# Mixer halves of the first two output row tiles computed ahead of the attention halves

## The chip, the core and the metric

The kernel runs on one core of a Trainium2 chip. The metric is the time of one execution on the device, in microseconds (us); lower is better. TensorE (PE) multiplies matrices and writes its results into PSUM, which this kernel uses as eight banks of 128 x 512 float32. VectorE (DVE) and ScalarE (ACT) read PSUM and work on tiles in SBUF, the on-chip memory. SyncE's queue (SP) issues all the transfers of the part that matters here. PEld in the profile is TensorE loading the stationary operand of the next matmul.

## The reference

A sequence of 2048 rows of width 1024 goes through two branches, and a gate for each row mixes them:

```
g = sigmoid((x * gate_w).sum(-1))                 # one number for each row
a = attention(x) @ wo                             # 32 heads of 32, 8 keys at distance 2
z = gelu(x @ w_in)                                # 3584 columns, halves z1 and z2 of 1792
b = (z1 * (w_sp @ layernorm(z2) + b_sp)) @ w_out
out = g * a + (1 - g) * b
```

The inputs and the output are bfloat16. The attention of a row sees itself and seven earlier rows, 2, 4, ... 14 back.

## The kernel before

The kernel writes its instructions in an order that is laid down by hand; each engine works through its own list in that order, and semaphores hold an instruction until what it reads is there. The PE work comes in stages: z2 for the gate and layer norm (L232), the queries, keys and values (L447), z1 (L483), and then the stages around the change.

`g_chunk(c)` (L491 to L505) computes the spatial mixing for a chunk of 512 rows: for each of 14 feature tiles 16 matmuls into a bank `ps` (L497), a copy by ACT into one of three `gsb` buffers (L501), the bias added and the product with z1 taken by DVE (L502, L503). The product replaces z1 in the tile `z1c`, of which there are two, for even and odd chunks.

`final_chunk(c)` (L507 to L533) makes the output of the four row tiles `a` of 128 rows in a chunk. For each half of 512 columns it runs the **attention half**, 8 matmuls of the transposed attention output `oT` with `wo` into a bank `psa` (L519), and then the **mixer half**, 14 matmuls of `z1c` with `w_out` into a bank `psb` (L523). ACT scales psa by the gate into `asb` (L526), DVE adds psb times one minus the gate (L527), and the finished row tile is stored (L533). All banks come from one pool of eight under one tag. There are three `oT` buffers; `load_oT(a + 2)` (L369) is issued when row tile `a` begins, and the first three are loaded before the stage.

The attention runs on DVE, beside PE's matmuls, in eight groups of four heads. A small planner called `Beat` counts PE's columns as time and puts DVE's attention steps and some transfers in between by due times: `beat.run(cols)` advances its clock and issues what has come due, and `beat.flush(t)` issues all that is due up to t. The last steps of the attention in that plan are: the store of the last two head groups into the scratch tensor `o_d` in device memory (`store_o`, L326), the four loads of `wo` (`load_wo`, L366), and the first three transposed reads of `o_d` into the `oT` buffers.

The end of the program is written out as

```
g_chunk(0)
...
g_chunk(1)
...
beat.flush(1e9)
final_chunk(0)
load_z1c(2)
g_chunk(2)
final_chunk(1)
load_z1c(3)
g_chunk(3)
final_chunk(2)
final_chunk(3)
```

Here `load_z1c(c)` (L400) reads the z1 of a chunk into its tile, and `load_wsp` (L397) the spatial weights of a chunk, into one of two buffers. `w_out` is read by one transfer ahead of `g_chunk(0)` (L539).

Of the kernel before, what the change touches and what calls it, by code (L numbers as in the profile page):

```python
# [10 lines left out]
F32 = mybir.dt.float32  # L11
BF = mybir.dt.bfloat16

P = 128
S = 2048
D = 1024
KT = D // P
# [9 lines left out]
NF = FH // P  # L27
# [24 lines left out]
def kernel(  # L52
# [13 lines left out]
    nc = tc.nc  # L66
# [5 lines left out]
    psum = ctx.enter_context(tc.tile_pool(name="psum", bufs=8, space=bass.MemoryType.PSUM))  # L72
# [4 lines left out]
    def reg(off, n):  # L77
        return arena[:, off:off + n]
# [20 lines left out]
    for jh in range(2):  # L99
        for w in range(W):  # L100
            n = min(8, max(0, 14 - 2 * w - 8 * jh))
            if n > 0:
# [3 lines left out]
    g_s = sm.tile([P, 16], F32, name="g_s")  # L106
    gl_s = sm.tile([P, 16], F32, name="gl_s")
    omg = sm.tile([P, 16], F32, name="omg")
# [17 lines left out]
    w_out_sb = reg(X_OFF, NF * D).rearrange("p (f n) -> p f n", f=NF)  # L126
# [5 lines left out]
    wo_sb = reg(A_OFF, KT * D).rearrange("p (k n) -> p k n", k=KT)  # L132
    oT_slots = [reg(A_OFF + 8192 + r * 1024, 1024).rearrange("p (k t) -> p k t", k=KT) for r in range(3)]
    ob_slots = [reg(A_OFF + 11264 + r * 1024, 1024) for r in range(3)]
    asb_slots = [reg(A_OFF + 14336 + r * 1024, 1024).bitcast(F32) for r in range(2)]
# [10 lines left out]
    z1c_slots = [reg(CD_OFF + 8192, 7168).rearrange("p (f t) -> p f t", f=NF),  # L146
                 reg(EF_OFF + 8192, 7168).rearrange("p (f t) -> p f t", f=NF)]
# [49 lines left out]
    beat = Beat()  # L197
# [170 lines left out]
    def load_oT(a):  # L368
        sync.dma_start_transpose(oT_slots[a % 3], o_d[a * P:(a + 1) * P, :])  # L369
# [26 lines left out]
    def load_wsp(c, aa):  # L396
        sync.dma_start_transpose(wsp_slots[c % 2][:, :, aa, :], wsp_v[4 * c + aa])  # L397
# [41 lines left out]
    for ch in range(NCH):  # L439
# [3 lines left out]
        for j in range(NJ):  # L443
            ps = psum.tile([P, 512], F32, name="ps", tag="ps")
            for kt in range(KT):
                lhsT = _sub_ap(xT_flat, kt * S + j, [[NJ, P]])
                nc.tensor.matmul(ps[:].rearrange("p (t c) -> p t c", t=4), lhsT, wgt[:, :, kt, :],  # L447
                                 start=(kt == 0), stop=(kt == KT - 1))
# [25 lines left out]
    for f in range(NF):  # L474
# [5 lines left out]
        for c in range(4):  # L480
            ps = psum.tile([P, 512], F32, name="ps", tag="ps")
            for kt in range(KT):
                nc.tensor.matmul(ps[:], w1[:, kt, (f % 4) * P:(f % 4 + 1) * P], xT[:, kt, 512 * c:512 * (c + 1)],  # L483
                                 start=(kt == 0), stop=(kt == KT - 1))
# [6 lines left out]
    def g_chunk(c):  # L491
        wsp = wsp_slots[c % 2]
        z1c = z1c_slots[c % 2]
        for f in range(NF):
# [9 lines left out]
            beat.on_vector(0.85)  # L504
            beat.run(16 * 512)  # L505

    def final_chunk(c):  # L507
        z1c = z1c_slots[c % 2]
        for aa in range(4):
            a = 4 * c + aa  # L510
            oT = oT_slots[a % 3]
            ob = ob_slots[a % 3]
            if a > 0 and a + 2 < 16:
                load_oT(a + 2)
            last = a == 15
            for n0, nw in ((0, 512), (512, 256), (768, 256)) if last else ((0, 512), (512, 512)):
                psa = psum.tile([P, 512], F32, name="psa", tag="ps")
                for kt in range(KT):
                    nc.tensor.matmul(psa[:, 0:nw], oT[:, kt, :], wo_sb[:, kt, n0:n0 + nw],  # L519
                                     start=(kt == 0), stop=(kt == KT - 1))  # L520
                psb = psum.tile([P, 512], F32, name="psb", tag="ps")
                for f in range(NF):
                    nc.tensor.matmul(psb[:, 0:nw], z1c[:, f, aa * P:(aa + 1) * P], w_out_sb[:, f, n0:n0 + nw],  # L523
                                     start=(f == 0), stop=(f == NF - 1))
                asb = asb_slots[n0 // nw % 2][:, 0:nw]
                nc.scalar.activation(asb, psa[:, 0:nw], ACT.Copy, scale=g_s[:, a:a + 1])  # L526
                nc.vector.scalar_tensor_tensor(ob[:, n0:n0 + nw], psb[:, 0:nw], omg[:, a:a + 1], asb,  # L527
                                               ALU.mult, ALU.add)
                beat.run((KT + NF) * nw)
                if last:  # L530
                    sync.dma_start(out2[a * P:(a + 1) * P, n0:n0 + nw], ob[:, n0:n0 + nw])
            if not last:
                sync.dma_start(out2[a * P:(a + 1) * P, :], ob)  # L533
# [9 lines left out]
    g_chunk(1)  # L543
    for aa in range(4):
        load_wsp(3, aa)
    beat.flush(1e9)
    final_chunk(0)
    load_z1c(2)
    g_chunk(2)
# [6 lines that stand above are left out]
# [29 lines left out]
```

## Time and profile before

| what | value |
|---|---|
| median of 3 runs | 720.5 us (719.03 to 721.43) |
| profiled execution, its own time | 722.27 us |
| span of the profiled execution | 720.5 us |
| mean granted TensorE clock | 0.995 |
| PE busy | 711.8 us, 99% of the span |
| DVE, ACT busy | 413.7 us, 246.3 us |
| matmuls of g_chunk (L497) | 896, 193.9 us |
| attention halves psa (L519) | 264 in the records, 62.3 us |
| mixer halves psb (L523) | 462 in the records, 103.4 us |

The profile records one execution. The span goes from its first to its last instruction; the execution's own time also holds what lies around the span. The table of groups gives for each kind of instruction how many there were, their busy time, the mean of one, and the idle time of the engine just before them with what ended it. The chain of waits is followed back from the last instruction, at each step to what released it. The granted clock is 1.00 at full speed.

### The profile page before, as it was taken

The page shows a single profiled execution, that of the slowest core. Times are in us where ns is not written, and L with a number is a line of the kernel's source. Part 1 is how long each engine was busy: PE and PEld are TensorE (multiplying, and loading weights), DVE is VectorE, ACT ScalarE, POOL GpSimd, SP SyncE. Part 2 cuts the span into 40 slices and gives each one's busy share as a digit, 9 for nine tenths or more (in the row PEclk, how much of TensorE's full clock was granted, in tenths as well). Part 3 has the DMA queues.
Part 4 walks back from the last instruction along what each step waited for, and adds up shares of the span by engine and source line. Part 5 has one row for each costly group of instructions (what it writes and reads, how often), then busy time and mean ns, then how long its engine had stood idle before and what let it go on. Part 6 is the DMA issues. An engine that isn't in the chain of part 4 may idle for free. (4 is left out here: it accounts for less than half of the span.)

```text
span 720.5 us, 8378 instructions
## 1 busy us (share of the span) xinstructions
PE 711.8 (99%) x3372; PEld 365.8 (51%) x3372; DVE 413.7 (57%) x429; ACT 246.3 (34%) x451; POOL 14.0 (2%) x23
## 2 busy tenths in 40 slices
PE   8999999999999999999999999899999999999998
PEld 4466666666655554444444444344444444444444
DVE  0000589999999999999999999311222112221111
ACT  4433544435379885343421211111112111111111
POOL 1000000000000212000000000000000000000000
PEclk9999999999999999999999999999999999999999
DMA  9984974876672035955369580862400113002310
GB/s 234 191 180 106 250 199 110 200 182 171 177 229 82 0 114 120 258 199 172 142 195 313 189 172 1 226 139 58 132 1 0 42 47 131 1 1 58 60 45 30
DMA packets 176759, 92.89 MB, mean 129 GB/s; under 512 B 145104, under 2 KB 166992, under 8 KB 176208
## 3 DMA queue, kind: packets, MB, share of 16 engines
q1 hardware_dynamic: 176720, 92.36, 48.0%
q8 instruction: 26, 0.43, 0.2%
q14 instruction: 13, 0.11, 0.0%
HBM read 47.71 MB, written 28.38 MB: 106 GB/s over the span
## 5 line engine op out<-in xcount | busy, mean ns | idle before, releaser
L497 PE MATMUL ps<-arena 128*128 128x512 bf16 x896 | 193.9, 379 | 0.0
L447 PE MATMUL ps<-arena 128*128 128x512 bf16 x768 | 165.9, 379 | 0.0
L497 PEld LDWEIGHTS <-arena 128*128 128x128 bf16 x896 | 87.7, 98 | 105.7
L447 PEld LDWEIGHTS <-arena 128*128 128x128 bf16 x768 | 110.7, 144 | 55.1
L523 PE MATMUL psb<-arena 128*128 128x512 bf16 (+1 forms) x462 | 103.4, 376 | 0.0
L275 DVE TENSOR_TENSOR arena<-arena 128x8192 bf16<-128x8192 bf16 x16 | 70.8, 4424 | 51.9 <-DMA arena<-k_d 51.6
L527 DVE SCALAR_TENSOR_TENSOR arena<-psb,omg,arena 128x512 bf16<-128x512 f32 (+1 forms) x33 | 24.2, 735 | 131.9 <-PE psb L523 131.9
L232 PE MATMUL ps<-arena 128*128 128x512 bf16 (+1 forms) x512 | 97.3, 352 | 1.1 <-DMA arena<-in_B_w_in_dram 1.1
L483 PE MATMUL ps<-arena 128*128 128x512 bf16 x448 | 96.9, 379 | 0.0
L501 ACT CAST arena<-ps 128x512 bf16<-128x512 f32 x56 | 32.9, 587 | 162.0 <-PE ps L497 129.4
L450 ACT CAST arena<-ps 128x512 bf16<-128x512 f32 x96 | 55.9, 589 | 92.7 <-PE ps L447 87.1
L278 DVE TENSOR_TENSOR arena<-arena 128x4096 bf16<-128x4096 bf16 (+1 forms) x64 | 77.5, 1210 | 1.9
L232 PEld LDWEIGHTS <-arena 128*128 128x128 bf16 x512 | 50.1, 98 | 48.0 <-issue 1.2
L523 PEld LDWEIGHTS <-arena 128*128 128x128 bf16 x462 | 45.6, 99 | 52.8 <-issue 2.2
L308 DVE TENSOR_TENSOR arena<-arena,att_A 128x8192 bf16<-128x8192 bf16 x16 | 70.7, 4421 | 0.2
L483 PEld LDWEIGHTS <-arena 128*128 128x128 bf16 x448 | 43.8, 98 | 52.7
L526 ACT ACTIVATE arena<-psa,g_s 128x512 f32<-128x512 f32 (+1 forms) x33 | 22.3, 675 | 128.7 <-PE psa L519 128.7
L519 PE MATMUL psa<-arena 128*128 128x512 bf16 (+1 forms) x264 | 62.3, 380 | 3.3 <-DMA arena<-o_d 3.3
L502 DVE TENSOR_TENSOR arena<-arena 128x512 bf16<-128x512 bf16 x56 | 23.6, 422 | 72.1 <-ACT arena L501 72.1
L485 ACT ACTIVATE arena<-ps 128x512 bf16<-128x512 f32 x56 | 32.2, 597 | 51.5 <-PE ps L483 42.4
L519 PEld LDWEIGHTS <-arena 128*128 128x128 bf16 x264 | 26.1, 99 | 34.1 <-issue 5.4
L237 ACT ACTIVATE arena<-ps 128x512 bf16<-128x512 f32 (+1 forms) x64 | 34.3, 539 | 24.9 <-PE ps L232 24.8
(54 smaller groups left out, 256.7 us busy)
## 6 DMA issues: line engine op xcount, KB each, us to landing
arena<-k_d SPq DMA_DIRECT2D x8, 960.0 KB, 7.6
arena<-v_d SPq DMA_DIRECT2D x8, 960.0 KB, 4.9
z_d<-arena SPq DMA_DIRECT2D x14, 512.0 KB, 3.7
arena<-z_d SPq DMA_DIRECT2D x4, 1792.0 KB, 7.2
arena<-in_A_wqkv_dram SPq DMA_DIRECT2D x24, 256.0 KB, 4.6
arena<-in_B_w_in_dram SPq DMA_DIRECT2D x4, 1024.0 KB, 6.7
q_d<-arena SPq DMA_DIRECT2D x32, 128.0 KB, 2.3
k_d<-arena SPq DMA_DIRECT2D x32, 128.0 KB, 2.3
```

The costliest lines, as they stand in the source:

```text
L232: nc.tensor.matmul(ps[:, 0:N], xT[:, kt, i * P:(i + 1) * P], w2[:, kt, ZC * c:ZC * c + N], start=(kt == 0), stop=(kt == KT - 1))
L237: nc.scalar.activation(z2[:, i, ZC * c:ZC * c + n], ps[:, 0:n], ACT.Gelu_apprx_tanh, accum_out=s1[:, 4 * i + c:4 * i + c + 1])
L275: TT(prod.rearrange("p (w j c) -> p w j c", w=W, j=8, c=C), in0, in1, ALU.mult)
L278: return lambda: TT(pv[:, :, 0:half], pv[:, :, 0:half], pv[:, :, half:2 * half], ALU.add)
L308: TT(prod.rearrange("p (w j d h) -> p w j d h", w=W, j=8, d=DH, h=HG), in0, in1, ALU.mult)
L447: nc.tensor.matmul(ps[:].rearrange("p (t c) -> p t c", t=4), lhsT, wgt[:, :, kt, :], start=(kt == 0), stop=(kt == KT - 1))
L450: nc.scalar.copy(st[:, j % 4, :], ps[:])
L483: nc.tensor.matmul(ps[:], w1[:, kt, (f % 4) * P:(f % 4 + 1) * P], xT[:, kt, 512 * c:512 * (c + 1)], start=(kt == 0), stop=(kt == KT - 1))
L497: nc.tensor.matmul(ps[:], z2[:, i, f * P:(f + 1) * P], wsp[:, i, :, :].rearrange("p a t -> p (a t)"), start=(i == 0), stop=(i == 15))
L501: nc.scalar.copy(gsb, ps[:])
L519: nc.tensor.matmul(psa[:, 0:nw], oT[:, kt, :], wo_sb[:, kt, n0:n0 + nw], start=(kt == 0), stop=(kt == KT - 1))
L523: nc.tensor.matmul(psb[:, 0:nw], z1c[:, f, aa * P:(aa + 1) * P], w_out_sb[:, f, n0:n0 + nw], start=(f == 0), stop=(f == NF - 1))
```

## The change

The body of `final_chunk` is split into three functions: `attn_mm` (the attention half), `mixer_mm` (the mixer half) and `combine` (ACT's scaling and DVE's addition). In `final_chunk(0)` alone, the mixer halves of row tiles 0 and 1, four of them, are computed first, each into a bank of its own, and kept in a dictionary. The loop over the row tiles then runs as before, but takes the mixer half from the dictionary where it has one. So the first four attention halves follow each other on PE, each with its combine. From row tile 2 on, attention and mixer halves alternate as they did. The call `beat.flush(1e9)` stands behind these four mixer halves and no longer in front of `final_chunk(0)`.

```diff
+    def mixer_mm(a, n0, nw):
+        z1c = z1c_slots[a // 4 % 2]
+        aa = a % 4
+        psb = psum.tile([P, 512], F32, name="psb", tag="ps")
+        for f in range(NF):
+            nc.tensor.matmul(psb[:, 0:nw], z1c[:, f, aa * P:(aa + 1) * P], w_out_sb[:, f, n0:n0 + nw],
+                             start=(f == 0), stop=(f == NF - 1))
+        beat.run(NF * nw)
+        return psb
...
     def final_chunk(c):
...
+        first = {}
+        if c == 0:
+            for a in range(2):
+                for n0 in (0, 512):
+                    first[a, n0] = mixer_mm(a, n0, 512)
+            beat.flush(1e9)
+        for a in range(4 * c, 4 * c + 4):
             ob = ob_slots[a % 3]
             if a > 0 and a + 2 < 16:
                 load_oT(a + 2)
             last = a == 15
             for n0, nw in ((0, 512), (512, 256), (768, 256)) if last else ((0, 512), (512, 512)):
...
-                beat.run((KT + NF) * nw)
+                psa = attn_mm(a, n0, nw)
+                psb = first[a, n0] if (a, n0) in first else mixer_mm(a, n0, nw)
+                combine(a, n0, nw, psa, psb)
...
-    beat.flush(1e9)
     final_chunk(0)
```

`attn_mm` holds the lines of the old loop for psa, and `combine` those for `asb` and `ob`; `beat.run` is now called after each half with that half's columns.

## The prediction

> **What bounds the kernel now.** I read the page first: how full TensorE (PE) is, and the chain of work that ended last.
>
> ```profile
> span 720.5 us, 8378 instructions
> PE 711.8 (99%) x3372; PEld 365.8 (51%) x3372; DVE 413.7 (57%) x429; ACT 246.3 (34%) x451; POOL 14.0 (2%) x23
> ...
> PE 35%; DVE 10%; DMA 2%; issue 0%; DVEq 0%
> ...
> L519 PE MATMUL psa<-arena 128*128 128x512 bf16 (+1 forms) x264 | 62.3, 380 | 3.3 <-DMA arena<-o_d 3.3
> ```
>
> PE is busy 711.8 of 720.5 us. A change that only reorders PE's work can win no more than its idle time plus what it computed at a lower clock. The last line shows the longest idle spell that a releaser is named for: 3.3 us, before the attention matmuls psa (L519), ended by a DMA out of o_d. The next view is the chain of waits in order of time, around that place (start, length, what):
>
> ```profile
> 452.38 0.69 DVE arena L311
> 453.07 0.03 DVE arena L502
> 453.10 6.13 DMA o_d<-arena
> 459.23 0.02 issue
> 459.24 6.28 DMA arena<-o_d
> 465.53 0.09 issue
> 465.62 3.57 PE psa L519 x8
> 469.19 4.28 PE psb L523 x14
> 473.47 1.73 PE psa L519 x8
> 475.20 3.02 PE psb L523 x14
> ```
>
> The last attention group leaves VectorE (DVE) at 453.1, is stored to o_d (6.13 us), read back transposed (6.28 us), and only then does the first psa start, at 465.62. The first psa and psb then take 3.57 and 4.28 us, and every later pair 1.73 and 3.02. Third view: stretches, with the busy times of PE, PEld, DVE, ACT and POOL, the granted clock, the DMA share and GB/s:
>
> ```profile
> 459.00:462.00 3.00, 3.00 (x16) 1.27 (x13) 0.85 (x2) 0.46 (x1) 0.00 (x0) 1.00 1.05 408
> 462.00:465.00 3.00, 0.29 (x2) 0.00 (x0) 0.85 (x2) 0.59 (x1) 0.00 (x0) 0.96 1.12 339
> 465.00:468.00 3.00, 2.38 (x6) 0.90 (x7) 0.00 (x0) 0.00 (x0) 0.00 (x0) 0.50 1.06 202
> 468.00:471.00 3.00, 3.00 (x8) 1.06 (x7) 0.00 (x0) 0.69 (x1) 0.00 (x0) 0.50 1.20 208
> 471.00:474.00 3.00, 3.00 (x14) 1.31 (x13) 0.42 (x1) 0.00 (x0) 0.00 (x0) 0.90 1.15 248
> 474.00:506.00 32.00, 32.00 (x150) 14.56 (x149) 4.84 (x7) 4.81 (x7) 0.00 (x0) 1.00 0.28 70
> ```
>
> PE stops at 462.29 (32.54 us of g_chunk matmuls from 429.75 in the timeline). The granted clock falls to 0.50 while it stands, and is back near 471.6 (0.90 over 471 to 474 is 0.6 us of half clock). So the wait costs twice: the idle time, and a slow stretch behind it.
>
> **The change part by part.**
>
> *The hole that goes.* Idle: 465.62 - 462.29 = 3.33 us. Slow stretch: psa 3.57 - 1.73 = 1.84, psb 4.28 - 3.02 = 1.26, together 3.10 us. Sum 6.43 us. Counted the other way: final_chunk(0) runs from 462.29 to 506.71, 44.42 us; its eight pairs at full clock are 8 x (1.73 + 3.02) = 38.00; the difference is 6.42.
>
> *What fills it.* Four psb groups of 14 matmuls move ahead of the first psa: 4 x 3.02 = 12.08 us of PE work that exists anyway, so no PE time is added. In the changed program's instruction order these 56 matmuls stand between the last g_chunk(1) matmul and the first psa; PE has as many rows as before. They would run from 462.29 to 474.37 if their inputs are there.
>
> *Inputs of the moved matmuls.* w_out was issued at 383.84 and took 18.0 us: 401.8, 60 us early. The z1c tile of chunk 0 is finished by g_chunk(0)'s multiplies (L503). DVE works in order, and between 430.1 and 463.4 the timeline shows 13 L503, all but one of chunk 1's 14, so chunk 0's were done by 430, 32 us early. The first moved load's two DMA waits in the changed program are for w_out and for the z1c load that preceded those multiplies, none for wo or oT. Cost: nothing.
>
> *Where the stall goes; who is late next.* The first psa is now wanted at 474.37, and its oT landed at 465.53: 8.8 us of cover. The four wo loads were issued before it, the last at 457.6, with a median of 6.6 to landing: 464.2. The next three attention halves follow without a mixer half between them, so oT 1 is wanted at 474.37 + 2 x 1.73 = 477.83 and oT 2 at 481.29. They were issued at 461.3 and 464.5 and took 5.9 and 3.9 us: 467.2 and 468.4, with 10 and 13 us of cover. If that cover were gone, each us beyond it would be a us of PE time.
>
> *PSUM banks.* Four of the eight hold finished mixer halves until their combine. The banks they take were last used by g_chunk(1) tiles which ACT copied out at one per 3.45 us, the very last at 462.32 + 0.59 = 462.9. The first combine ends about 474.37 + 1.73 + 0.27 + 0.69 (ACT) + 0.75 (DVE) = 477.8; tile 2, the first to want these banks again, begins at 481.29. In the run of four psa one is made each 1.73 us and the combine needs 0.69 on ACT and 0.75 on DVE, so both keep up. No wait.
>
> *Queues.* The moved flush has nothing left to issue: the changed program's SP list has the same transfers in the same order (o_d store, wo, three oT, the last w_sp tiles, then the output stores), and ACT's and DVE's lists are the same too. The first output store waits for tile 0's second combine, about 474.37 + 2 x 1.73 + 1.71 = 479.5, against 479.12 before; behind it on SP stands the load of oT 3. It needs 3.2 us, so lands near 483.5, and is wanted after tile 2's pairs, at 481.29 + 9.50 = 490.79. DVE's first combine waits 4.3 us longer than before (473.58 against 477.1 at its start), with only later combines behind it. Cost: nothing.
>
> *After that.* final_chunk(0) would end at 462.29 + 38.00 = 500.29 and not 506.71. From there PE runs to its end at 717 with no idle spell in the list of waits, its transfers hang on PE's own progress and move with it, so nothing downstream gives the 6.42 back. Reloading z1c makes DVE wait 4.2 us there, beside PE's matmuls; that stays the same.
>
> *How long is the cold stretch worth?* The row says half clock from about 464.8 to 471.6, 6.8 us, costing 3.10. [...] The row decides, since it is this very hole. [...]
>
> The price of the changed order itself is not in the trace. Below nothing is excluded, since the matmuls are the same ones and run at full clock already after 474; the nearest row for the other end is the hole itself, 6.4 us again, if PE were to stop once more. I take nothing, as the alternating halves and the g_chunk matmuls both run without gaps, and keep the other end for rival C.
>
> The sum against the profiled execution: span 720.5 - 6.4 = 714.1; its own time 722.27, 1.77 outside the span, becomes 715.8. The median of the runs is 720.5 (719.03 to 721.43), so it becomes 714.1.
>
> **The rivals.**
>
> *A: the half clock is not the idle time's doing but that of the transfers* (DMA share above 1 from 459 to 474), and the slow stretch of 6 us stays. Only 3.33 would be won: 717.2. For it: the low clock coincides with full DMA engines. Against: from 459 to 462 the DMA share is 1.05 at 408 GB/s with clock 1.00, and it falls only after PE has stood.
>
> *B: a wait returns in part.* The combines, the banks or oT 1 and 2 stop PE for 1 to 4 us inside final_chunk(0): 715 to 718. Against: the smallest cover above is 3.4 us.
>
> *C, slower: the oT transfers land later because PE now works through them.* PE idled while they flowed; if 56 matmuls fetching their operands slow the transfers, the first psa waits anew after 474.37, PE stands, and the clock falls again. This eats the whole gain when the stall reaches 6.43 - 3.10 = 3.33 us, that is with landing at 477.7, 18.5 us after issue instead of 6.28. At 22 us it would be 481.2: 6.9 + 3.1 - 6.4 = 3.6 us slower, 724.1. For it: w_out took 18.0 us. Against: that is one of 3.6 MB, and the slowest oT in the view of these loads took 7.8.
>
> That the change does not do what it says is ruled out by the instruction order.
>
> **How the numbers follow.** Forecast, idle and slow stretch both gone: 0.84, 714.1. A: 0.05. B: 0.08. C: 0.03. A measurement of this kernel can tell about 0.3% from no change, 2.2 us, so faster means under 718.3. Faster: the forecast, A and most of B, 0.94; same 0.03 (the rest of B and the edge of C); slower 0.03. The range takes the spread of the three runs, about 1.2 us either way; below it adds 0.5 us for edges of the hole that the modelled ends of matmuls may blur, above 1.3 us for the nearer half of B: 712.4 to 716.6. A, B's far end and C lie outside, with the tails of the spread less than 2 in 10.
>
> **What would show it.** In the profile after: no idle before psa with a DMA as releaser; psb running on from the last g_chunk matmul, 56 in about 12.1 us; then four psa groups of 1.73; granted clock 1.00 from 459 to 474; the next g_chunk starting near 500.3. A clock of 0.50 without idle would mean A; gaps before psa or psb in the 470s and 480s, B; a wait on o_d near 474, C. A span above 717 would make the prediction wrong.

## The result and the profile after

The changed kernel takes 715.86 us (median of 6 runs, 715.36 to 716.16) against 720.03 us of the kernel before (6 runs on the same chip, 718.89 to 721.43). The ratio is 0.9942, 95% interval 0.9929 to 0.9956: 4.2 us faster. The profiled execution has a span of 714.1 us and an own time of 715.91.

The page of the kernel after, its span, its busy times, and the chain that ended last, by engine:

```profile
span 714.1 us, 8323 instructions
PE 706.3 (99%) x3321; PEld 365.5 (51%) x3372; DVE 413.9 (58%) x429; ACT 246.1 (34%) x451; POOL 14.0 (2%) x23
...
PE 98%; DMA 1%; issue 0%; SPq 0%; DVE 0%; DVEq 0%
```

Before, the chain left PE at the hole and went back through two transfers to DVE, and PE had 35% of the span in it. Now it stays on PE almost to the start. The timeline of PE's instructions after, around the place of the hole (start, length, what):

```profile
429.82 32.54 PE L497 MATMUL ps<-arena 128*128 128x512 bf16 x147
462.19 12.25 PE L520 MATMUL psb<-arena 128*128 128x512 bf16 x55
474.28 8.80 PE L510 MATMUL psa<-arena 128*128 128x512 bf16 x39
482.91 3.19 PE L520 MATMUL psb<-arena 128*128 128x512 bf16 x14
485.93 1.89 PE L510 MATMUL psa<-arena 128*128 128x512 bf16 x8
...
497.16 3.19 PE L520 MATMUL psb<-arena 128*128 128x512 bf16 x14
500.18 5.13 PE L497 MATMUL ps<-arena 128*128 128x512 bf16 x22
```

psb follows the last g_chunk matmul, five attention halves follow the four moved mixer halves, and g_chunk(2) starts at 500.18, where the same view of before has 506.55. (A few matmul records are missing, so 55 and 39 stand for 56 and 40.) The stretches of the same kernel, with the granted clock as the third number from the end:

```profile
462.00:465.00 3.00, 3.00 (x16) 1.34 (x14) 0.85 (x2) 0.58 (x1) 0.00 (x0) 1.00 1.11 344
465.00:468.00 3.00, 3.00 (x15) 1.36 (x14) 0.00 (x0) 0.00 (x0) 0.00 (x0) 1.00 1.04 200
468.00:471.00 3.00, 3.00 (x15) 1.37 (x14) 0.00 (x0) 0.00 (x0) 0.00 (x0) 1.00 1.12 202
471.00:474.00 3.00, 2.95 (x14) 1.37 (x14) 0.00 (x0) 0.00 (x0) 0.00 (x0) 1.00 1.67 179
```

PE is full, the clock is 1.00, and the transfers are as dense as before. Between the two profiled executions the span falls by 6.4 us, to the tenth what was forecast for it. The medians differ by only 4.2. The experiments had to say where the other 2.2 us are.

### The profile page after: what moved, and what is told of

Read it like the earlier page. It is cut to its first block, busy times and chain, and to the rows that moved or that the text cites. A ratio compares the mean times of both kernels' runs of the same rounds, so it can differ in the third digit from the quotient of the medians.

```text
span 714.1 us, 8323 instructions
## 1 busy us (share of the span) xinstructions
PE 706.3 (99%) x3321; PEld 365.5 (51%) x3372; DVE 413.9 (58%) x429; ACT 246.1 (34%) x451; POOL 14.0 (2%) x23
## 4 chain that ended last, share of the span: by engine, by line
PE 98%; DMA 1%; issue 0%; SPq 0%; DVE 0%; DVEq 0%
PE ps L497 27%; PE ps L447 23%; PE ps L232 14%; PE ps L483 13%; PE psb L520 13%; PE psa L510 8%; DMA arena<-in_B_w_in_dram 1%; SPq L405 0%; DVE arena L528 0%; DVEq L528 0%
## 5 line engine op out<-in xcount | busy, mean ns | idle before, releaser
L520 PE MATMUL psb<-arena 128*128 128x512 bf16 (+1 forms) x455 | 100.9, 372 | 0.3
L510 PE MATMUL psa<-arena 128*128 128x512 bf16 (+1 forms) x259 | 59.6, 372 | 0.3
```

Of the source, the lines that this page charges most:

```text
L510: nc.tensor.matmul(psa[:, 0:nw], oT_slots[a % 3][:, kt, :], wo_sb[:, kt, n0:n0 + nw], start=(kt == 0), stop=(kt == KT - 1))
```

## The experiments

The theory: what the change gives is the time that PE stands idle before the first attention half, plus whatever the half clock behind it costs in that execution; the changed order itself costs nothing. The rivals are A (the transfers lower the clock), B (banks, combines or loads stop PE elsewhere), C (late loads of oT eat the gain), and that the runs of the kernel before differ for reasons all over the kernel. Spans are own times less 1.8 us in every run.

### e1_again: the kernel before, run by run

No edit.

> The kernel before, unchanged, to see the span and the granted clock of each run. Theory (the idle spell is fixed by the chain store, load; the slow stretch behind it varies in length): every run has the 3.3 us of idle time, and the runs differ by their half-clock time: where the mean granted clock is lower, the span is longer, by about half of the half-clock time. A clock of 0.995 goes with 720.5, 0.998 with about 718.5. Own times 718.9 to 722.3, a spread of 3 us, against 0.8 us for the changed kernel, whose clock is 1.00 throughout. Rival (the runs spread for another reason, along the whole kernel): spans and clocks do not go together, and the changed kernel's narrow spread is chance.

Measured: 720.61 us (12 runs, 719.0 to 723.29), ratio to the other runs of before 1.0008 (0.9996 to 1.002). With the runs of the kernel before that stood beside the later experiments there are 75 executions with span and mean granted clock:

| mean granted clock | runs | span, median | span, lowest to highest |
|---|---|---|---|
| 0.999 and 1.000 | 26 | 717.45 us | 716.6 to 718.2 |
| 0.997 and 0.998 | 45 | 719.0 us | 718.2 to 721.5 |
| 0.995 | 4 | 720.9 us | 720.3 to 721.8 |

So clock and span go together: the more half clock, the longer the span, and no run stands at 0.996. Inside a group the spans still spread over 1.5 to 3.3 us, so the rival, another reason for the spread, holds for a part of it. The profile that the prediction was made from, 720.5 us at 0.995, is of the rarest one. The profile of e1 is of the middle one. Its chain of waits, to be read beside that of before:

```profile
458.85 6.28 DMA arena<-o_d
465.13 0.09 issue
465.22 2.80 PE psa L519 x8
468.01 3.80 PE psb L523 x14
471.81 1.73 PE psa L519 x8
473.54 3.02 PE psb L523 x14
```

The same 6.28 us load ends the hole, but the slow stretch costs (2.80 - 1.73) + (3.80 - 3.02) = 1.85 us here and not 3.10. The same kernel's stretches show why:

```profile
465.50:466.00 0.50, 0.50 (x4) 0.22 (x3) 0.00 (x0) 0.00 (x0) 0.00 (x0) 1.00 0.61 143
466.00:466.50 0.50, 0.50 (x3) 0.15 (x1) 0.00 (x0) 0.00 (x0) 0.00 (x0) 0.54 1.47 103
466.50:467.00 0.50, 0.50 (x3) 0.20 (x2) 0.00 (x0) 0.00 (x0) 0.00 (x0) 0.50 0.90 170
...
469.00:469.50 0.50, 0.50 (x3) 0.16 (x2) 0.00 (x0) 0.00 (x0) 0.00 (x0) 0.54 1.27 287
469.50:470.00 0.50, 0.50 (x4) 0.26 (x3) 0.00 (x0) 0.00 (x0) 0.00 (x0) 1.00 1.29 286
```

The slices in between read 0.50 and those around them 1.00, so 0.54 over half a microsecond is taken as 0.46 us of half clock: the clock fell at 466.04 and came back at 469.46, after 3.42 us. In the profile of before, cut as finely:

```profile
464.50:465.00 0.50, 0.00 (x0) 0.00 (x0) 0.00 (x0) 0.00 (x0) 0.00 (x0) 0.79 1.28 280
...
471.00:472.00 1.00, 1.00 (x4) 0.39 (x3) 0.00 (x0) 0.00 (x0) 0.00 (x0) 0.69 1.26 271
```

It fell at 464.79 and came back at 471.62: 6.83 us, twice 3.42. An estimate from these two profiles: 3.42 us of half clock take 3.42 x 0.5 / 718.8 = 0.0024 off the mean clock, and 6.83 us take 0.0047, so runs with none, 3.42 or 6.83 us would show 1.000, 0.998 and 0.995. That fits the three groups, whose medians lie 1.55 and 1.9 us apart, where half of 3.42 is 1.7. What the other runs had is not shown, as they left no profile.

### e2_fill14: the hole filled with work that is thrown away

```diff
     beat.flush(1e9)
+    warm_up(14)
     final_chunk(0)
```

> The order of the kernel before, with 14 matmuls on a zero tile put into the hole ahead of the first attention half; their result is not used. They take 14 x 0.216 = 3.02 us of the 3.33 us that PE stood idle. Theory (standing idle lowers the clock): the first psa still starts near 465.6, but at full clock, the slow stretch is gone: a span of 720.5 - 3.1 = 717.4, own time about 719.1, or 3.3 us over the changed kernel, and a spread of the runs under 1 us. Rival A (the transfers lower the clock): the slow stretch stays, and the time is that of the kernel before.

Measured: 719.2 us (11 runs, 718.82 to 720.9), ratio 0.9992 (0.9984 to 1.0001), clock 0.999 or 1.000 in every run, as against 26 of 75 of the kernel before. The time is the 719.1 that was expected, the spread is not: 2.1 us and not under 1, by one run. Against the median of before, which already contains many runs with little or no half clock, that is not a clear gain. What tells is the clock of the runs and the profile. PE's timeline and two stretches of this kernel:

```profile
462.13 3.19 PE L92 MATMUL pw<-warm 128*128 128x512 bf16 x14
465.27 1.89 PE L519 MATMUL psa<-arena 128*128 128x512 bf16 x8
466.99 3.19 PE L523 MATMUL psb<-arena 128*128 128x512 bf16 x14
```

```profile
465.00:468.00 3.00, 3.00 (x15) 1.30 (x14) 0.00 (x0) 0.69 (x1) 0.00 (x0) 1.00 1.02 188
468.00:471.00 3.00, 3.00 (x16) 1.37 (x14) 0.71 (x1) 0.00 (x0) 0.00 (x0) 1.00 1.25 208
```

The first attention half starts where it did, under the same transfers, at full clock. Rival A is out: with the idle time filled, the clock is 1.00 under a DMA share of 1.02 and 1.25. And 719.2 is 3.3 us over the changed kernel, about the idle time alone.

### e3_one_half: one mixer half ahead and not four

```diff
-            for a in range(2):
-                for n0 in (0, 512):
-                    first[a, n0] = mixer_mm(a, n0, 512)
+            first[0, 0] = mixer_mm(0, 0, 512)
```

> Only the mixer half of row tile 0, columns 0 to 511, is computed ahead, the other three stay where they were. Theory (the hole is 3.33 us, and whatever fills it does): one half fills 3.02 us, 0.3 us of idle time stay and no slow stretch: span 714.1 + 0.3 = 714.4, own time 716.2. Rival (each half held ahead gives its share of the gain): a quarter of the gain, span about 718.9. Rival B (holding four banks costs): this is faster than the changed kernel by what the banks cost.

Measured: 716.4 us (6 runs, 715.73 to 718.34), ratio 0.9956 (0.9943 to 0.9969). One half gives nearly the whole gain, as its 3.02 us fill nearly the whole hole. A quarter of the gain would have been 718.9 of span, about 720.7 of own time. The profiled execution is the highest of the six, 716.6 of span. Its g_chunk(1) ended 2.3 us late, at 464.55; the delay is in its first 12 us and so has nothing to do with the edit. The same stretch in it (6 matmuls) and in the profile after (14):

```profile
6.00:9.00 3.00, 2.51 (x6) 0.84 (x6) 0.00 (x0) 1.66 (x2) 0.00 (x0) 1.00 1.00 350
...
6.00:9.00 3.00, 2.91 (x14) 1.35 (x14) 0.00 (x0) 1.35 (x2) 0.00 (x0) 1.00 1.02 361
```

In e3 a matmul took 2.51 / 6 = 0.42 us of PE's busy time there, in the profile after 2.91 / 14 = 0.21: PE worked at half pace, and the granted clock of the view says 1.00 all the same. So the mean granted clock of that run does not hold all of its slow time, and a late start like this is one way in which runs of equal clock differ. Around the hole the execution shows:

```profile
464.55 3.02 PE psb L520 x14
467.58 0.07 issue
467.65 3.61 PE psa L510 x16
```

Here the gap left is 0.07 us, where 0.3 was expected. That the other three halves are needed is not shown by the time; they are margin.

### e4_all_chunks: the same order in all four chunks

```diff
-        if c == 0:
-            for a in range(2):
+        if True:
+            for a in range(4 * c, 4 * c + 2):
```

> The mixer halves of the first two row tiles of every chunk are computed ahead, four times and not once. In chunks 1 to 3 there is no hole to fill. Theory (the changed order costs PE nothing): the same span as the changed kernel, 714.1, own time 715.9. Rival B (four banks held, and four attention halves in a run, stop PE for a while): the three further chunks each add that price, 1 us each would give 718.9 own time.

Measured: 716.14 us (5 runs, 715.17 to 716.38), ratio 0.9947 (0.9935 to 0.9958), span of the profiled execution 714.4. Three further chunks in the changed order add nothing that can be told from the changed kernel's 715.36 to 716.16. Chunk 2 in its chain of waits:

```profile
635.29 12.09 PE psb L520 x56
647.38 8.63 PE psa L510 x40
656.01 3.02 PE psb L520 x14
659.03 1.73 PE psa L510 x8
```

56 and 40 matmuls without a pause, in a chunk without a hole: holding four of the eight banks costs PE nothing here. Rival B is out.

### e5_fill5 and e8_fill10: shorter holes

The edit of e2 with `warm_up(5)` and `warm_up(10)`.

> The order of the kernel before, with 5 matmuls on a zero tile in the hole, result not used: 5 x 0.216 = 1.08 us, so PE stands 2.25 us and not 3.33 before the first attention half, which still starts near 465.6. Theory (a spell must last for some time until the clock falls; in the profile before it fell about 2.4 us after the last matmul): the clock falls in few or none of the runs, own time near that of the kernel with 14 such matmuls, about 719. Rival (any gap of this kind costs the whole slow stretch): as the kernel before, its mean 720 and its spread of 3 us.

> As the kernel with 5 matmuls on a zero tile in the hole, but with 10: 2.16 us of the hole filled, so PE stands 1.0 to 1.2 us. With about 3.2 us of idle time half or more of the runs showed a mean granted clock of 0.998 or less, with about 2.3 us 5 of 12, with 0.2 us none of 11. [...] Rival (the chance falls in proportion to the gap, whatever its length): 1 in 5 runs or so at 0.998 or below, those near 720.8.

With 5, measured 719.49 us (12 runs), ratio 0.9985 (0.9974 to 0.9996). PE stood 2.45 us in the profile, and the clock fell all the same in 5 of 12 runs (0.997; 718.8 to 719.5 of span), among them the profiled one. So my expectation of few or none was wrong. Two stretches of it:

```profile
465.50:466.00 0.50, 0.50 (x2) 0.23 (x3) 0.00 (x0) 0.00 (x0) 0.00 (x0) 0.67 0.77 171
...
469.00:469.50 0.50, 0.50 (x3) 0.20 (x2) 0.00 (x0) 0.50 (x1) 0.00 (x0) 0.92 1.25 264
```

The clock fell at 465.67, 0.2 us after PE had restarted at 465.48, and came back at 469.08, 3.41 us later. In the profile of before PE had stood 464.79 - 462.29 = 2.5 us when it fell.

With 10, PE stood 0.92 us; measured 719.19 us (12 runs, 718.72 to 722.15), ratio 0.999 (0.9975 to 1.0004). One run of 12 shows 0.997, at 722.15, the others 0.999 and 1.000. Between no run and the rival's one in five that does not decide. What that one run was slow for stays open, and so does a run of 721.75 at 1.000. The counts of runs at 0.998 and below are thus 49 of 75 with some 3.2 us of idle time, 5 of 12 with 2.45, 1 of 12 with 0.92 and none of 11 with almost none.

### e6_late and e7_before_late: the price of a late load

Both kernels issue the first three loads of oT behind the last spatial weights:

```diff
-        for a in range(3):
-            beat.at(t + 8.0, lambda a=a: load_oT(a))
...
     for aa in range(4):
         load_wsp(3, aa)
+    beat.flush(1e9)
+    for a in range(3):
+        load_oT(a)
```

> The changed kernel, with the three first loads of oT issued behind the four loads of the last spatial weights on SP. Those took 9.3 us of SP before and begin when g_chunk(1) has ended, so oT 0 is issued near 472 and lands 4 to 6 us later, 476 to 478 or a little more, where it is wanted at 474.3. Theory: each us beyond 474.3 is a us that PE stands idle, 2 to 4 us, and once this comes near 3 us the clock falls and adds up to 3 us: own time 718 to 722.5, about what the kernel before takes. Rival (the cover is larger than the four mixer halves, or the transfers are hidden anyway): the time of the changed kernel, 715.9.

> The kernel before with the same late loads of oT, nothing computed ahead. Theory: oT 0 lands at 476 to 478, so PE stands for 14 to 16 us from 462.3 and not 3.3, and the slow stretch follows: own time 720 + 11 to 13 = 731 to 733. The four mixer halves, 12.1 us, are then worth 10 to 13 us and not 4 to 6: what the change gives is the smaller of the hole and the 12.1 us put into it, and the slow stretch only where the hole is closed. Rival (the mixer halves give a fixed gain): 4 us over the changed kernel with the same late loads.

Measured: the changed kernel with late loads 718.85 us (12 runs, 717.07 to 720.72), ratio to the kernel before 0.9975 (0.9961 to 0.9989); the kernel before with late loads 732.5 us (4 runs, 731.77 to 733.76), ratio 1.0161 (1.0145 to 1.0178). Both lie where they were expected. The chain of waits of the first, then of the second:

```profile
472.23 2.75 PE psb L518 x12
474.99 2.00 issue
476.98 8.15 PE psa L508 x37
```

```profile
472.62 3.89 DMA arena<-o_d
476.51 0.09 issue
476.60 3.57 PE psa L517 x8
480.18 3.55 PE psb L521 x14
```

With four halves ahead PE stands 2.00 us in the profile. The view names no releaser there, but oT 0 was issued at 473.06, 3.92 us before PE went on at 476.98. The clock reads 1.00 in every stretch from 459 to 483; 4 of the 12 runs show 0.998, at 718.0 to 718.9 of span, and were not profiled. In e7, without them, PE stood 14.29 us, and the slow stretch cost (3.57 - 1.73) + (3.55 - 3.02) = 2.37 us more. So the same change is worth 732.5 - 718.85 = 13.65 us here, and is not a fixed gain. The two profiles differ by 730.8 - 716.8 = 14.0 us of span: 14.29 - 2.00 = 12.29 of idle time, about the 12.1 us of matmuls put ahead, and 2.37 of slow stretch, less 0.57 because g_chunk(1) ended that much later in e6 (462.90 against 462.33). The price that rival C put on a late load, a microsecond of PE for each microsecond past the cover, is what e6 shows for 2.00 us: PE stood from 474.99, when the mixer halves had ended, to 476.98, when the first psa started. Its reason for a late load is not: from the issue of oT 0 to the first psa it took 3.92 us in e6, where PE worked for 1.93 of them, and 3.98 us in e7, beside an idle PE.

## Why the prediction was right, and its one wrong step

The range, 712.4 to 716.6, held 715.86, and the direction was right. By its own steps:

- **The hole, 6.43 us, goes whole.** Right for the profiled execution: 720.5 to 714.1 of span, no idle time, clock 1.00.
- **Nothing is late next.** Right: no transfer releases PE there; oT 3 and the output stores follow as laid out, g_chunk(2) starts at 500.2 for a forecast 500.29, and e4 shows that order and banks cost nothing. (The smallest cover, called 3.4 us under rival B, is 481.29 - 477.8 = 3.5 by the prediction's own numbers; nothing hangs on it.)
- **The queues.** Right: the last combine of tile 0 let its store go at 479.43 for a forecast 479.5.
- **Rivals A, B, C.** A is refuted by e2, B by e4. For C, e6 shows the price of a late load, but PE's work did not make the load late: oT 0 took 6.3 us to land beside it, as before, and e6 against e7 says the same.
- **The median, 714.1: 1.8 us too low.** The step that failed is "The median of the runs is 720.5, so it becomes 714.1". It took the whole hole of one execution off the median of others. That execution's own time was 722.27, above all of the runs beside it (719.03 to 721.43). Both figures stand in the prediction, but it draws no conclusion from them. Its half clock lasted 6.83 us and cost 3.10 us; the largest group of runs has the clock of e1, where it lasted 3.42 us and cost 1.85. Put on its own time the sum was right (715.8, and the changed kernel's median is 715.86). For the median, the three groups less the changed kernel's 714.1 give gains of 3.35, 4.9 and 6.8 us; weighted with 26, 45 and 4 runs that is 4.5 us, against 4.2 measured in the first comparison.
- **The range was held with luck.** 715.86 is 1.76 us above 714.1, more than the 1.2 us that the range takes for the spread of the runs. It lies inside because of the 1.3 us added above for the nearer half of rival B, and B did not occur.
- **The cold stretch priced by one row.** The prediction took 3.10 us because the row was of this very hole. It was right for that execution: with the 3.33 us of idle time it makes up the 6.4 us between the two profiles. In e1, in whose group of clocks 45 of the 75 runs lie, it cost 1.85 us, and 26 runs show 0.999 or 1.000.

The narrow spread of the changed kernel, 0.8 us against 2.5 in the same comparison, goes with the clock in part: its six runs show 0.999 or 1.000, where those of the kernel before fall into the three groups. The rest is not shown; e2, at full clock in every run, still spread over 2.1 us.

## What to carry to other kernels

Where PE waits for a chain of transfers, look for matmuls of the next stage whose inputs are already there, and put at least as much of them ahead as the wait is long; more is margin against a later load (e6, 718.85 us where e7 took 732.5), and cost nothing that could be told with four of the eight banks held (e4, 716.14 against 715.86 us); more than four was not tried. Before a hole is priced by one profile, compare that execution's own time and granted clock with the other runs: the half clock behind the hole lasted 6.83 us in one execution of this kernel and 3.42 in another, and an execution above all the others is not the median. Sum against the profiled execution's own time and carry over to the median only what the median run has.

## What the runs showed of the hardware

- The clock fell 2.50 us after PE's last matmul in the profile of before (464.79 - 462.29) and 5.15 us after it in e7 (467.46 - 462.31), both times while PE stood. In e1 it fell 0.82 us after PE had restarted from 3.04 us of idle time (466.04 - 465.22), and in e5 0.19 us after PE had restarted from 2.45 us (465.67 - 465.48). So the time from PE's last matmul to the fall was not the same in these four: 2.50, 5.15, 3.86 and 2.64 us.
- An idle spell of 2.45 us was enough in the profile of e5, where 5 of 12 runs show 0.997. One of 2.00 us in the profile of e6 left the clock at 1.00, and one of 0.92 us in that of e8 left a mean of 0.999. In e7 the clock still read 1.00 in the stretch up to 467.00, after 4.69 us. From what length on an idle spell lowers the clock is not shown; the one run of e8 at 0.997 and the four of e6 at 0.998 left no profile.
- The clock stayed down for 3.42 us in e1, 3.41 in e5, 6.83 in the profile of before and 13.68 in e7 (467.46 to 481.14): close to once, once, twice and four times 3.42. The two ends in e7, between which every stretch reads 0.50:

```profile
467.00:468.00 1.00, 0.00 (x0) 0.00 (x0) 0.00 (x0) 0.00 (x0) 0.00 (x0) 0.73 1.25 201
...
480.00:483.00 3.00, 3.00 (x13) 1.27 (x12) 0.00 (x0) 0.69 (x1) 0.00 (x0) 0.81 0.00 0
```

- In e1 and e5 PE was busy through all of the half clock. In the profile of before its first 0.83 us were idle (465.62 - 464.79), in e7 its first 9.14 us (476.60 - 467.46). From PE's restart to the return of the full clock it took 4.24 us in e1, 3.60 in e5, 6.00 in the profile of before and 4.54 in e7. What sets the length is not shown.
